# Clustered attention and a squared-ReLU feed-forward on one core: first pair on other banks and a second load queue, query-half ends given precedence, down products in another order

## The chip, the core and the metric

The kernel runs on one core of a Trainium2 chip. The metric is the device time of one execution, in microseconds (us). The core has five engines with queues of their own, which are served in order and meet only through semaphores: TensorE (PE; its weight loads are shown apart as PEld), VectorE (DVE), ScalarE (ACT), GpSimd (POOL) and SyncE (SP), which here only issues DMAs. TensorE writes its results to PSUM, a small memory of eight banks.

## The reference

Attention over 4 batches, 8 heads, 768 positions, 64 dimensions. A query sees a key only where both lie nearest to the same of 16 centroids of their head. The result, heads side by side, is the input (3072 x 512) of a feed-forward with a squared ReLU.

```python
q_assign = np.argmax(np.einsum('bhsd,hcd->bhsc', q_n, c_n), axis=-1)
k_assign = np.argmax(np.einsum('bhsd,hcd->bhsc', k_n, c_n), axis=-1)
mask = q_assign[:, :, :, None] == k_assign[:, :, None, :]
scores = scale * np.matmul(q, k.transpose(0, 1, 3, 2))
scores = np.where(mask, scores, -1000000000.0)
...
attn = np.exp(scores)
attn = attn / (np.sum(attn, axis=-1, keepdims=True) + 1e-09)
out = np.matmul(attn, v)
...
h = x @ w_in           # (3072, 512) @ (512, 2048)
r = np.maximum(h, 0.0)
g = r * r
return g @ w_out       # (3072, 2048) @ (2048, 512)
```

The inputs are float32. `_n` marks vectors divided by their length.

## The kernel before

**Pairs.** Two heads of a batch make a pair; there are 16 pairs (`NG`), four (`HP`) per batch. `load_qk` (L91) brings q and k of a pair with two DMAs each, one per head; all DMAs are issued on SP. `prep` (L324) prepares a pair in seven items: `turn` (L232) three times, which transposes four of the twelve 128x128 blocks of q and k on TensorE and has ACT copy them to `qkT`; `logits` (L250), the products with the normed centroids `cnT`; `route` (L263), which transposes the logits (`lt`) and finds each position's cluster on DVE (`mx`, `best`, `ids`); and two items that make the mask. In batch 0 (pairs 0 to 3) the mask is a one-hot matrix `oh`, transposed on TensorE by `turn_onehot` (L298) and added to the scores as a further product. In the other batches `spread` (L313) makes `qid` and the mask is a comparison on DVE after the exponential (L370).

**Units.** A pair has two query halves of 384 positions, a half three units of two key blocks. `scores` (L343) computes a unit's scores on TensorE and has ACT take the exponential (L364, tile `ex`); two units later (`LAG`) `times_v` (L386) multiplies by the values (`av`) and, in batch 0 and the first half, by ones (`sm`). Elsewhere POOL adds the exponentials up (`acc`), and `finish` (L403) makes `sm` from that with two small products. `finish` then takes the reciprocal (L420) on DVE, writes the half's part of `xT` (L421) and notes in `good` (L426) whether the sums were usable.

**PSUM.** `ps_sc` holds one tile of scores (four banks), `ps_av` two banks (tag `av`), `ps_f` two banks (tag `f`), which every transpose, logit and feed-forward product of the first stage shares.

**Feed-forward.** The weights are rounded while attention runs (`round_weights`, L131: two ACT, three DVE and one POOL operation for each of 32 pieces). For the halves in `PLAIN` (batches 0 and 1) `ffn` (L434) yields one product at a time, and the loop over units fills TensorE's queue with them. Batches 2 and 3 go through `ffn_pair` (L465) after attention, one batch at a time: seven products of quarters in place of eight, first for the up product (L519, width 384), then for the down product (L550, width 256, three tiles `i`). `combine` (L482) runs the seven in the order 1, 6, 2, 7, 5, 4, 3 and has DVE add them into the four results. For the down product, operand `g_s` of numbers 5 and 6 is made on DVE from the squared activations (L540, L473). Each tile `i` gives two blocks of the output, h=0 and h=1, each stored with one DMA of 256 KB (L561).

**Order.** The code is written for a scheduler that keeps program order except where `high_priority(offset)` moves instructions ahead, and that chooses among ready instructions of an engine by priority. So an engine's queue is not simply the program's order. `together` (L79) keeps products that can share TensorE's array side by side. The main loop (L606 on) goes over the 48 units: `scores`, `times_v` of two units before, weight rounding, fill, items of the next pair's `prep`, and `finish` where a half ends.

**End.** `check_sums` (L659) condenses `good` to one flag, after batch 2's `ffn_pair`. All engines load the flag (L698) and branch (L699) to a slow general path, which these inputs never take.

Of the kernel before, what the change touches and what calls it, by code (L numbers as in the profile page):

```python
# [8 lines left out]
F32 = mybir.dt.float32  # L9
# [15 lines left out]
def kernel(  # L25
# [50 lines left out]
    def bank(name, shape):  # L76
        return ps_f.tile(shape, F32, name=name, tag="f")

    def together(products, offset=2000):  # L79

        products = iter(products)
        nc.tensor.matmul(**next(products))  # L82
        with tc.high_priority(offset=offset):
            for product in products:
                nc.tensor.matmul(**product)  # L85
# [5 lines left out]
    def load_qk(pair):  # L91
        if pair >= NG:
            return
        b, hp = divmod(pair, HP)
        raw[pair] = []
        for name, src in (("q_raw", q), ("k_raw", k)):
            t = loads.tile([P, NCH, 2 * D], F32, name=name, tag="qk")
            for e in range(2):
                nc.sync.dma_start(
                    t[:, :, D * e : D * (e + 1)],  # L100
                    src[b, 2 * hp + e].rearrange("(p j) d -> p j d", p=P),
                )
            raw[pair].append(t)
# [53 lines left out]


    cen = once_early.tile([P, D], F32, name="cen")
    nc.sync.dma_start(cen, centroids.rearrange("h c d -> (h c) d"))  # L160
    load_qk(0)
    load_qk(1)

# [20 lines left out]
    def centroids_norm():  # L184
        sq = once_early.tile([P, D], F32, name="cen_sq")
        ss = const.tile([P, 1], F32, name="cen_ss")
        nc.vector.tensor_tensor(out=sq, in0=cen, in1=cen, op=ALU.mult)
        nc.vector.reduce_sum(out=ss, in_=sq, axis=AX.X)
        nc.vector.tensor_scalar_max(out=ss, in0=ss, scalar1=1e-30)
        nrm = const.tile([P, 1], F32, name="cen_nrm")  # L190
        nc.scalar.sqrt(nrm, ss)
        warm = once_early.tile([P, 1], F32, name="warm")
        nc.scalar.activation(out=warm, in_=nrm, func=ACT.Exp, scale=0.0)
        for _ in range(2):
            r = small.tile([P, 1], F32, name="cen_r")
            nc.vector.reciprocal(out=r, in_=nrm)
            twice = small.tile([P, 1], F32, name="cen_twice")
            nc.vector.scalar_tensor_tensor(
                out=twice, in0=ss, scalar=r, in1=nrm, op0=ALU.mult, op1=ALU.add
            )  # L200
            nc.vector.tensor_scalar_mul(out=nrm, in0=twice, scalar1=0.5)
        nc.vector.tensor_scalar_add(out=nrm, in0=nrm, scalar1=1e-6)
        rden = const.tile([P, 1], F32, name="cen_rden")
        nc.vector.reciprocal(out=rden, in_=nrm)
        row_i = const.tile([P, 1], I32, name="row_i")
        nc.gpsimd.iota(row_i, pattern=[[0, 1]], base=0, channel_multiplier=1)
        nc.vector.tensor_scalar(
            out=row_i, in0=row_i, scalar1=C, scalar2=None, op0=ALU.bitwise_and
        )
        odd = const.tile([P, 2], F32, name="odd")  # L210
        nc.vector.tensor_scalar(
            out=odd[:, 1:2], in0=row_i, scalar1=1.0 / C, scalar2=None, op0=ALU.mult
        )
        nc.vector.tensor_scalar(
            out=odd[:, 0:1], in0=odd[:, 1:2], scalar1=-1.0, scalar2=1.0, op0=ALU.mult, op1=ALU.add
        )
        for e in range(2):
            nc.vector.tensor_scalar(
                out=cn[:, e], in0=cen, scalar1=rden, scalar2=odd[:, e : e + 1],
                op0=ALU.mult, op1=ALU.mult,  # L220
            )
        pt = bank("pt", [P, P])
        nc.tensor.transpose(out=pt, in_=cn.rearrange("p e d -> p (e d)"), identity=ident)
        nc.vector.tensor_copy(out=cnT, in_=pt)

# [23 lines left out]

    def logits(pair):  # L250
        hp = pair % HP
        lg = bank("lg", [P, TB])
        together(
            dict(
                out=lg[32 * g : 32 * g + 32], lhsT=cnT[:, 2 * C * hp : 2 * C * (hp + 1)],
                rhs=qkT[pair][:, NB * g : NB * (g + 1)], start=True, stop=True,
            )
            for g in range(4)
        )
        lgs[pair] = rbp.tile([P, TB], F32, name="lgs", tag="rb")  # L260
        nc.scalar.copy(out=lgs[pair], in_=lg)
# [3 lines left out]
            number(pair)  # L265

    def number(pair):
        lt = bank("lt", [P, NB, P])
        src = lgs.pop(pair)
        for i in range(NB):  # L270
            nc.tensor.transpose(out=lt[:, i], in_=src[:, i * P : (i + 1) * P], identity=ident)
        n = NB * P // C
        lt = lt.rearrange("p i (g c) -> p (i g) c", c=C)
        mx = small.tile([P, n], F32, name="mx")
        nc.vector.reduce_max(out=mx, in_=lt, axis=AX.X)
        best = once.tile([P, n, C], BF16, name="best", tag="b")
        nc.vector.tensor_tensor(
            out=best, in0=lt, in1=mx.unsqueeze(2).to_broadcast([P, n, C]), op=ALU.is_ge
        )

        nc.vector.tensor_tensor(
            out=best, in0=best, in1=order.unsqueeze(1).to_broadcast([P, n, C]), op=ALU.mult
        )
        ids[pair] = idp.tile([P, NB, 4, 2], F32, name="ids")
        first = ids[pair].rearrange("p i g e -> p (i g e)")
        nc.vector.reduce_max(out=first, in_=best, axis=AX.X)
        if pair < HP:
            nc.vector.tensor_tensor(
                out=oh.rearrange("p i g e c -> p (i g e) c")[:, :, 0:C], in0=best,
                in1=first.unsqueeze(2).to_broadcast([P, n, C]), op=ALU.is_equal,  # L290
            )
            qid[pair] = [None, idp.tile([P, 2, S], BF16, name="ohT", tag="qid")]
        else:
            qid[pair] = [small.tile([P, NB, 2, 2], BF16, name="ids_b"),
                         idp.tile([P, 2, 2, TB], BF16, name="qid", tag="qid")]
            nc.vector.tensor_copy(out=qid[pair][0], in_=ids[pair][:, :, 0:2])

    def turn_onehot(pair, which):  # L298
        pt = ps_f.tile([P, NCH, P], BF16, name="po", tag="f")
        for c in range(NCH):  # L300
            nc.tensor.transpose(
                out=pt[:, c],
                in_=oh[:, c % NB, 2 * which + c // NB].rearrange("p e c -> p (e c)"),
                identity=ident_b,
            )
        dst = qid[pair][1][:, which]
        src = pt.rearrange("p c n -> p (c n)")
        if which == 0:
            nc.scalar.copy(out=dst, in_=src)
        else:  # L310
            nc.scalar.activation(out=dst, in_=src, func=ACT.Copy, bias=-BIG, scale=BIG)
# [153 lines left out]
    def ffn_pair(pools, b):  # L465
# [6 lines left out]
        def sub(out, a, b, eng=nc.vector):  # L472
            eng.tensor_tensor(out=out, in0=a, in1=b, op=ALU.subtract)  # L473
# [5 lines left out]
        t3 = x[0][1]  # L479
        g = gp.tile([P, FT, 2, TB], F32, name="g")  # L480

        def combine(c, product, width):  # L482

            (c11, c12), (c21, c22) = c

            def add(j, *results):
                bank = bk(width)
                product(j, bank)
                for out, to in results:
                    nc.vector.tensor_tensor(out=out, in0=bank, in1=to, op=ALU.add)  # L490

            bank = bk(width)
            product(1, bank)
            nc.scalar.copy(out=c11, in_=bank)
            add(6, (c12, c11))
            add(2, (c11, c11))
            add(7, (c21, c12))
            add(5, (c22, c21), (c12, c12))
            bank = bk(width)
            product(4, bank)  # L500
            sub(c21, c21, bank)
            add(3, (c12, c12))

        for i in range(F2):
# [31 lines left out]
        for i in range(NB):  # L536
# [19 lines left out]

            osb = [later["out"].tile([P, DM], F32, name="osb") for _ in range(2)]
            c = [[osb[h][:, M2 * m : M2 * (m + 1)] for m in range(2)] for h in range(2)]
            combine(c, product, M2)
            for h in range(2):  # L560
                nc.sync.dma_start(out_view[b, h * NB + i], osb[h])  # L561

# [31 lines left out]
    to_round = iter(range(len(weights)))  # L596
    loaded = iter(range(len(weights)))
    centroids_norm()
    for item in prep(0):
        item()  # L600
    load_v(0)
    ahead = []
# [3 lines left out]
    for u in range(len(units) + LAG):  # L606
# [35 lines left out]
        fill_steps(share - share // 2)  # L642
        if done:
            pair, h = done
            finish(pair, h)
            b, hp = divmod(pair, HP)
            if h == 1:
                for d in (qkT, ids, qid):
# [40 lines left out]
    for b in range(B):  # L689
        if (b, 0) not in PLAIN:  # L690
            ffn_pair(pools, b)
            if w_sums is not None:
                w_sums = None
                check_sums()
    fast.close()
    keep.close()

    again = nc.values_load(flag[0:1, 0:1], min_val=0, max_val=1)  # L698
    with tc.If(again != 0):  # L699
        general_path(  # L700
            tc, q, k, v, out, w_in, w_out, cn, ident, order
# [186 lines left out]
```

## Time and profile before

| | |
|---|---|
| time, median of 3 runs | 1078.52 us (1078.18 to 1081.37) |
| the profiled run | 1078.8 us, span of its records 1076.7 us |
| granted TensorE clock, mean | 0.993 |
| attention with batches 0 and 1 of the feed-forward | 7.5 to about 775 us |
| `ffn_pair` of batch 2, of batch 3 | about 775 to 925 us, 925 to 1071 us |
| DMA: read, written | 37.26 MB, 6.29 MB |

In a list in order of time, each line gives start and duration in us, engine, line of the kernel, operation, what is written <- what is read, shapes and count; in brackets the idle time of the engine before it and what ended that wait. A name with a q (SPq) is the engine's instruction queue, where DMA issues and branches are found. Ends of products on TensorE are modelled, and one float32 product leaves two records.

### The profile page before, as it was taken

The numbers are of one execution on the slowest core, as the hardware profiler recorded it, in microseconds if no ns is written. First come the engines' busy times: TensorE is split into PE (matmuls) and PEld (weight loads), VectorE is DVE, ScalarE is ACT, GpSimd is POOL, SyncE is SP. The second block draws the span as 40 slices with busy tenths as digits, with TensorE's granted clock in tenths as the row PEclk, the third lists the DMA queues.
The fourth block names the chain that finished last, engine by engine and source line by source line (L and its number), as shares of the span: only waits on it lengthen the run. The fifth ranks groups of instructions, "written<-read, shape, count | busy, mean of one in ns | idle before, by whom it ended". The sixth has DMA issues, their size and how long they took to land. (4 is left out here: it accounts for less than half of the span.)

```text
span 1076.7 us, 11238 instructions
## 1 busy us (share of the span) xinstructions
PE 1044.7 (97%) x4419; PEld 546.6 (51%) x4419; DVE 698.1 (65%) x928; ACT 296.1 (28%) x402; POOL 371.9 (35%) x245
## 2 busy tenths in 40 slices
PE   6999899999999999999999999999999899999997
PEld 3444444444444443444443344443455688655886
DVE  2666988656798865689775578976476633366521
ACT  4656454222333331333322242321011100111000
POOL 1234865333444443345344334444143200132000
PEclk9999999999999999999999999999999999999999
DMA  8654332102011020201102000000000000000000
GB/s 211 168 165 133 113 97 80 44 10 54 12 43 44 1 54 10 54 15 30 44 1 54 10 25 2 15 1 11 19 1 0 1 20 20 20 0 1 10 30 23
DMA packets 63885, 44.36 MB, mean 41 GB/s; under 512 B 51536, under 2 KB 56656, under 8 KB 63824
## 3 DMA queue, kind: packets, MB, share of 16 engines
q1 hardware_dynamic: 63824, 43.56, 14.3%
q8 instruction: 37, 0.61, 0.2%
q14 instruction: 24, 0.20, 0.1%
HBM read 37.26 MB, written 6.29 MB: 40 GB/s over the span
## 5 line engine op out<-in xcount | busy, mean ns | idle before, releaser
L370 DVE SCALAR_TENSOR_TENSOR ex<-qid,ids,ex 128x384 f32<-128x384 bf16 x288 | 248.0, 920 | 96.1 <-ACT ex L364 96.0
L382 POOL TENSOR_TENSOR acc<-acc,ex 128x768 f32<-128x768 f32 x112 | 219.0, 1955 | 244.9 <-DVE ex L370 230.3
L364 ACT ACTIVATE ex<-sc 128x1536 f32<-128x1536 f32 x96 | 139.3, 1452 | 238.1 <-PE sc L85 238.1
L439 PE MATMUL ph<-xT,w_in 128*128 128x384 f32 x512 | 187.1, 503 | 4.0 <-DVE rb L420 3.9
L452 PE MATMUL po<-w_out,gT 128*128 128x512 f32 x384 | 180.4, 605 | 0.0
L85 PE MATMUL sc<-qkT 64*128 64x384 f32 x576 | 153.0, 504 | 0.0
L85 PE MATMUL av<-ex,v_raw 128*64 128x384 f32 x576 | 144.9, 496 | 0.0
L439 PEld LDWEIGHTS ph<-xT,w_in 128*128 128x128 f32 x512 | 91.3, 190 | 89.4 <-issue 37.5
L452 PEld LDWEIGHTS po<-w_out,gT 128*128 128x128 f32 x384 | 67.8, 190 | 88.2 <-issue 87.1
L420 DVE RECIPROCAL rb<-sm 128x384 f32<-128x384 f32 x32 | 81.6, 2550 | 25.4 <-PE sm L85 25.4
L82 PE MATMUL sc<-qkT 64*128 64x384 f32 x192 | 88.0, 539 | 1.5 <-ACT ex L364 1.5
L380 POOL TENSOR_TENSOR acc<-ex 128x768 f32<-128x768 f32 x28 | 52.5, 1876 | 97.2 <-DVE ex L370 92.3
L490 DVE TENSOR_TENSOR g<-bank,g 128x384 f32<-128x384 f32 x96 | 51.8, 554 | 48.1 <-PE bank L519 48.0
L82 PE MATMUL av<-ex,v_raw 128*64 128x384 f32 x192 | 82.5, 512 | 0.0
L85 PEld LDWEIGHTS sc<-qkT 64*128 64x128 f32 x576 | 66.3, 188 | 27.9 <-issue 4.2
L473 POOL TENSOR_TENSOR w_s<-w_in 128x256 f32<-128x256 f32 x16 | 12.5, 782 | 154.7 <-PE bank L519 154.7
L447 DVE TENSOR_TENSOR gT<-gT 128x384 f32<-128x384 f32 x64 | 58.9, 931 | 10.2 <-ACT gT L446 10.0
L490 DVE TENSOR_TENSOR osb<-bank,osb 128x256 f32<-128x256 f32 x36 | 14.7, 422 | 77.2 <-PE bank L550 70.9
L550 PE MATMUL bank<-w_out,g 128*128 128x256 f32 x288 | 64.4, 379 | 0.0
L85 PEld LDWEIGHTS av<-ex,v_raw 128*64 128x64 f32 x576 | 45.9, 136 | 34.4 <-issue 33.6
L446 ACT ACTIVATE gT<-ph 128x384 f32<-128x384 f32 x64 | 31.4, 491 | 109.6 <-PE ph L439 109.5
L550 PEld LDWEIGHTS bank<-w_out,g 128*128 128x128 f32 x288 | 54.7, 190 | 7.9
(118 smaller groups left out, 1188.1 us busy)
## 6 DMA issues: line engine op xcount, KB each, us to landing
w_raw<-in_moe_w_in_dram SPq DMA_DIRECT2D x16, 512.0 KB, 4.1
w_raw<-in_moe_w_out_dram SPq DMA_DIRECT2D x16, 512.0 KB, 3.4
v_raw<-in_v_dram SPq DMA_DIRECT2D x20, 384.0 KB, 3.7
q_raw<-in_q_dram SPq DMA_DIRECT2D x32, 192.0 KB, 3.5
k_raw<-in_k_dram SPq DMA_DIRECT2D x32, 192.0 KB, 3.9
out_dram<-osb SPq DMA_DIRECT2D x24, 256.0 KB, 2.0
cen<-in_centroids_dram SPq DMA_DIRECT2D x1, 32.0 KB, 1.9
```

The costliest lines, as they stand in the source:

```text
L82: nc.tensor.matmul(**next(products))
L85: nc.tensor.matmul(**product)
L364: last_exp[0] = nc.scalar.activation(out=t, in_=sc.rearrange("p i e n -> p (i e) n")[:, :, 0:TB], func=ACT.Exp, scale=SCALE).ins
L370: nc.vector.scalar_tensor_tensor(out=to, in0=qid[pair][1][:, h, e], scalar=ids[pair][:, ch % NB, 2 + ch // NB, e : e + 1], in1=to, op0=ALU ...
L380: nc.gpsimd.tensor_tensor(out=acc[pair, h], in0=t[:, 0:2], in1=t[:, 2:4], op=ALU.add)
L382: nc.gpsimd.tensor_tensor(out=acc[pair, h], in0=acc[pair, h], in1=t[:, 2 * i : 2 * i + 2], op=ALU.add)
L420: nc.vector.reciprocal(out=rb, in_=sm)
L439: nc.tensor.matmul(ph, lhsT=w_in[:, kk, f * P : (f + 1) * P], rhs=xT[b, h][:, kk], start=(kk == 0), stop=(kk == KT - 1),)
L447: nc.vector.tensor_tensor(out=gT[f], in0=gT[f], in1=gT[f], op=ALU.mult)
L452: nc.tensor.matmul(po, lhsT=gT[f][:, i * P : (i + 1) * P], rhs=w_out[:, f], start=(f == 0), stop=(f == FT - 1),)
L490: nc.vector.tensor_tensor(out=out, in0=bank, in1=to, op=ALU.add)
L550: nc.tensor.matmul(bank, lhsT=operands[j][0][:, f], rhs=operands[j][1][:, f], start=(f == 0), stop=(f == F2 - 1),)
```

## The change

- The first pair's PSUM tiles (centroid turn, logits, `lt`, one-hot turns) come from `ps_av` (`first_bank`) instead of `ps_f`; its three `turn` items stay on `ps_f`.
- The centroid load and the first pair's two k loads are issued on ACT's queue.
- The centroid transpose leaves `centroids_norm` and runs as `centroids_turned`, between the third `turn` item and `logits` of pair 0. The warming exponential reads `ss` instead of `nrm`.
- The first one-hot copy of pair 0 goes from ACT to DVE.
- `finish` is issued under `high_priority(offset=1000)`.
- `combine` takes a list `early`: for the down products, numbers 2 and 4 are issued right after number 1, and their results wait in their banks. The order is 1, 2, 4, 6, 7, 5, 3.
- The store of h=1 stands ahead of h=0's in the program, and the very last tile of h=0 is stored in two column halves.
- `values_load` of the flag moves to directly after `check_sums`.

```diff
@@ -76,6 +76,10 @@
     def bank(name, shape):
         return ps_f.tile(shape, F32, name=name, tag="f")

+    def first_bank(name, shape, dtype=F32):
+
+        return ps_av.tile(shape, dtype, name=name, tag="av")
+
     def together(products, offset=2000):

         products = iter(products)
@@ -96,7 +100,7 @@
         for name, src in (("q_raw", q), ("k_raw", k)):
             t = loads.tile([P, NCH, 2 * D], F32, name=name, tag="qk")
             for e in range(2):
-                nc.sync.dma_start(
+                (nc.scalar if pair == 0 and src is k else nc.sync).dma_start(
                     t[:, :, D * e : D * (e + 1)],
                     src[b, 2 * hp + e].rearrange("(p j) d -> p j d", p=P),
                 )
@@ -157,7 +161,7 @@


     cen = once_early.tile([P, D], F32, name="cen")
-    nc.sync.dma_start(cen, centroids.rearrange("h c d -> (h c) d"))
+    nc.scalar.dma_start(cen, centroids.rearrange("h c d -> (h c) d"))
     load_qk(0)
     load_qk(1)

@@ -189,8 +193,9 @@
         nc.vector.tensor_scalar_max(out=ss, in0=ss, scalar1=1e-30)
         nrm = const.tile([P, 1], F32, name="cen_nrm")
         nc.scalar.sqrt(nrm, ss)
+
         warm = once_early.tile([P, 1], F32, name="warm")
-        nc.scalar.activation(out=warm, in_=nrm, func=ACT.Exp, scale=0.0)
+        nc.scalar.activation(out=warm, in_=ss, func=ACT.Exp, scale=0.0)
         for _ in range(2):
             r = small.tile([P, 1], F32, name="cen_r")
             nc.vector.reciprocal(out=r, in_=nrm)
@@ -219,7 +224,9 @@
                 out=cn[:, e], in0=cen, scalar1=rden, scalar2=odd[:, e : e + 1],
                 op0=ALU.mult, op1=ALU.mult,
             )
-        pt = bank("pt", [P, P])
+
+    def centroids_turned():
+        pt = first_bank("pt", [P, P])
         nc.tensor.transpose(out=pt, in_=cn.rearrange("p e d -> p (e d)"), identity=ident)
         nc.vector.tensor_copy(out=cnT, in_=pt)

@@ -249,7 +256,7 @@

     def logits(pair):
         hp = pair % HP
-        lg = bank("lg", [P, TB])
+        lg = (bank if pair else first_bank)("lg", [P, TB])
         together(
             dict(
                 out=lg[32 * g : 32 * g + 32], lhsT=cnT[:, 2 * C * hp : 2 * C * (hp + 1)],
@@ -265,7 +272,7 @@
             number(pair)

     def number(pair):
-        lt = bank("lt", [P, NB, P])
+        lt = (bank if pair else first_bank)("lt", [P, NB, P])
         src = lgs.pop(pair)
         for i in range(NB):
             nc.tensor.transpose(out=lt[:, i], in_=src[:, i * P : (i + 1) * P], identity=ident)
@@ -296,7 +303,10 @@
             nc.vector.tensor_copy(out=qid[pair][0], in_=ids[pair][:, :, 0:2])

     def turn_onehot(pair, which):
-        pt = ps_f.tile([P, NCH, P], BF16, name="po", tag="f")
+        if pair == 0:
+            pt = first_bank("po", [P, NCH, P], BF16)
+        else:
+            pt = ps_f.tile([P, NCH, P], BF16, name="po", tag="f")
         for c in range(NCH):
             nc.tensor.transpose(
                 out=pt[:, c],
@@ -305,7 +315,9 @@
             )
         dst = qid[pair][1][:, which]
         src = pt.rearrange("p c n -> p (c n)")
-        if which == 0:
+        if which == 0 and pair == 0:
+            nc.vector.tensor_copy(out=dst, in_=src)
+        elif which == 0:
             nc.scalar.copy(out=dst, in_=src)
         else:
             nc.scalar.activation(out=dst, in_=src, func=ACT.Copy, bias=-BIG, scale=BIG)
@@ -479,26 +491,36 @@
         t3 = x[0][1]
         g = gp.tile([P, FT, 2, TB], F32, name="g")

-        def combine(c, product, width):
+        def combine(c, product, width, early=()):
+
+

             (c11, c12), (c21, c22) = c

-            def add(j, *results):
+            waiting = {}
+
+            def bank_of(j):
+                if j in waiting:
+                    return waiting[j]
                 bank = bk(width)
                 product(j, bank)
+                return bank
+
+            def add(j, *results):
+                bank = bank_of(j)
                 for out, to in results:
                     nc.vector.tensor_tensor(out=out, in0=bank, in1=to, op=ALU.add)

             bank = bk(width)
             product(1, bank)
             nc.scalar.copy(out=c11, in_=bank)
+            for j in early:
+                waiting[j] = bank_of(j)
             add(6, (c12, c11))
             add(2, (c11, c11))
             add(7, (c21, c12))
             add(5, (c22, c21), (c12, c12))
-            bank = bk(width)
-            product(4, bank)
-            sub(c21, c21, bank)
+            sub(c21, c21, bank_of(4))
             add(3, (c12, c12))

         for i in range(F2):
@@ -556,9 +578,12 @@

             osb = [later["out"].tile([P, DM], F32, name="osb") for _ in range(2)]
             c = [[osb[h][:, M2 * m : M2 * (m + 1)] for m in range(2)] for h in range(2)]
-            combine(c, product, M2)
-            for h in range(2):
-                nc.sync.dma_start(out_view[b, h * NB + i], osb[h])
+            last = b == B - 1 and i == NB - 1
+            combine(c, product, M2, early=(2, 4))
+
+            for h in (1, 0):
+                for cols in (slice(0, M2), slice(M2, DM)) if last and h == 0 else (slice(0, DM),):
+                    nc.sync.dma_start(out_view[b, h * NB + i][:, cols], osb[h][:, cols])

@@ -596,7 +621,9 @@
     to_round = iter(range(len(weights)))
     loaded = iter(range(len(weights)))
     centroids_norm()
-    for item in prep(0):
+    for i, item in enumerate(prep(0)):
+        if i == 3:
+            centroids_turned()
         item()
     load_v(0)
     ahead = []
@@ -642,7 +669,8 @@
         fill_steps(share - share // 2)
         if done:
             pair, h = done
-            finish(pair, h)
+            with tc.high_priority(offset=1000):
+                finish(pair, h)
             b, hp = divmod(pair, HP)
             if h == 1:
                 for d in (qkT, ids, qid):
@@ -692,10 +720,10 @@
             if w_sums is not None:
                 w_sums = None
                 check_sums()
+                again = nc.values_load(flag[0:1, 0:1], min_val=0, max_val=1)
     fast.close()
     keep.close()

-    again = nc.values_load(flag[0:1, 0:1], min_val=0, max_val=1)
     with tc.If(again != 0):
         general_path(
             tc, q, k, v, out, w_in, w_out, cn, ident, order
```

## Prediction

> **What bounds the kernel now.** I read the engine totals first, then the waits of TensorE, then the order of time around each long wait, and last the end of the run.
>
> ```profile
> span 1076.7 us, 11238 instructions
> PE 1044.7 (97%) x4419; PEld 546.6 (51%) x4419; DVE 698.1 (65%) x928; ACT 296.1 (28%) x402; POOL 371.9 (35%) x245
> ...
> PE pt L223 <- DVE cen_n L218: 7.5, 1, 7.5
> PE pb L318 <- DVE ids_b L296: 4.1, 7, 2.1
> PE ph L439 <- DVE rb L420: 3.9, 1, 3.9
> PE po L301 <- DVE oh L288: 3.5, 2, 2.3
> PE bank L550 <- DVE g_s L473: 3.2, 2, 2.9
> ...
> PE pb L318 <- DVE rb L420: 1.1, 2, 0.6
> ```
>
> TensorE is busy for 97% of the span, so the number and form of its products set the time; no edit changes those. The waits (engine, line, waited for: total us, times, longest) are what a reordering can win: all of TensorE's idle time is some 32 us, 7.5 of it at the start and 5.8 after its last product. The next lines, in order of time, place them.
>
> ```profile
> 2.57 1.34 SPq L99 DMA_DIRECT2D k_raw<-in_k_dram  x2
> 7.53 0.45 PE L223 MATMUL pt<-ident,cen_n 128*128 128x128 f32 x1 [7.53 <-DVE cen_n L218]
> 17.63 1.28 PE L301 MATMUL po<-ident_b,oh 128*128 128x128 bf16 x12 [2.26 <-DVE oh L288]
> 21.07 1.45 ACT L364 ACTIVATE ex<-sc 128x1536 f32<-128x1536 f32 x1 [0.17 <-PE sc L85]
> 32.99 0.84 PE L301 MATMUL po<-ident_b,oh 128*128 128x128 bf16 x12 [1.20 <-DVE oh L288]
> ...
> 126.80 2.54 DVE L420 RECIPROCAL rb<-sm 128x384 f32<-128x384 f32 x1
> 129.39 4.45 PE L439 MATMUL ph<-xT,w_in 128*128 128x384 f32 x8 [3.92 <-DVE rb L420]
> ...
> 854.18 5.35 PE L550 MATMUL bank<-w_t,g_s 128*128 128x256 f32 x16 [2.86 <-DVE g_s L473]
> 1001.54 3.72 PE L550 MATMUL bank<-w_t,g_s 128*128 128x256 f32 x16 [0.38 <-DVE g_s L473]
> 1070.91 0.42 DVE L490 TENSOR_TENSOR osb<-bank,osb 128x256 f32<-128x256 f32 x1 [3.03 <-PE bank L550]
> ...
> 854.00:856.00 2.00, 1.82 (x4) 1.51 (x5) 2.00 (x3) 0.00 (x0) 0.00 (x0) 0.53 0.00 0
> ```
>
> The first product runs at 7.53 because the centroid turn is at the head of TensorE's queue. At 854.18 the second product of the first down block waits 2.86 us for `g_s`, and sixteen records then take 5.35 us where the same sixteen take 3.62 elsewhere: the last line (columns: busy time of PE, weight load, DVE, ACT, POOL, then granted clock, DMA share, GB/s) shows a clock of 0.53 behind that wait.
>
> **What the Trainium skill says.** "TensorE: Matmul & The Clock Gate", Part 1, says that the clock halves after an idle window of some 3.4 us and comes back after a busy one, the windows running freely. The trace agrees: 0.5 from 854.1 to 857.5, so an idle of 2.86 us costs a further 5.35 - 3.62 = 1.73 us. "DMA: Bandwidth & Descriptors", Issuing engines are not separate DMA queues, says that issuing from several engines saves only issue time, as the same 16 DMA engines move all. The trace agrees in so far as these are full (mean busy share about 1.0 to 1.3 per us from 3 to 9 us, at 197 to 249 GB/s). The same page, Latency and other measured facts, puts a register load from memory at about 600 ns; the trace has 0.54 us for DVE's load of the flag at 1070.9.
>
> **The change, part by part.** I compared the queue of every engine in both kernels; durations are of the profiled execution, whose span is 1076.7 us. It was timed at 1078.8 us, and the three timed runs have 1078.18, 1078.52 and 1081.37. I work out savings on the span and take them off 1078.5.
>
> *Down products.* The queue becomes 1, 2, 4, 6, 7, 5, 3. Products 2 and 4 read raw quarters, so after product 1 there are two more blocks of 3.45 us (starts at 859.37 and 862.82) before product 6 needs `g_s`. Product 1 starts at 847.70, so product 6 comes at about 847.70 + 3 x 3.45 = 858.1; `g_s` ends at 852.92 + 1.21 = 854.1. The wait goes, and so does the cold clock. The in-place subtraction into the quarter that product 2 reads must follow that product (done about 854.6) and precede product 3, two blocks and more later. Saved: 2.86 + 1.73 at 854, and 0.38 + (3.72 - 3.62) at 1001, together 5.1 us. The additions are the same in number. Two banks are held longer, hidden by there being eight. Bounds 4 to 5.3.
>
> *First pair.* Removed ahead of the first transposes: the wait for `cen_n` (7.53) and one issue on SP (0.39 us for the centroids). Moved to ACT's queue: the centroid load and both k loads, 0.39 + 1.34 = 1.7 us of issue ahead of its table load, which was idle until 3.37; `cen_nrm` comes some 0.4 us later, but DVE's L201 no longer waits 1.10 us for `warm`, so `cen_n` is about 0.6 us earlier, and now nothing waits for it. On SP, the loads of pair 1 and v come forward 1.7 us, and with the DMA engines full they share with k. So I do not credit k with arriving earlier: it lands at 3.25 + 4.1 = 7.35 before (issue plus landing time) and I put it at 7.3, bounds 6.6 to 7.8. The six q transposes (1.3 us cold) now run in front of that, so k's are done at about 8.9 instead of 10.6. The centroid turn, four score products and the logits follow; the logits are copied at about 12.0 to 12.8 (13.25 before), and the first exponential, 21.07 before, comes at about 19.3: 1.8 saved. Two further gains: in the wait for `oh` TensorE now does pair 1's transposes, logits (1.0 us at 24.39) and `lt` (0.5), and nine of the twelve turns of pair 1's one-hot (0.6) come before the third scores, without the idle 1.20 at 32.99. Against this: those turns stand ahead of the second scores in TensorE's in-order queue and wait for a DVE chain with one more copy in it (`ohT`, about 0.8 us as on ACT), some 0.7 us. Sum: 1.8 + 1.0 + 0.5 + 0.6 + 1.2 - 0.7 = 4.4, rounded to 4.3; bounds 0 (k late, clock cold again) and 6. TensorE has no long wait between 33 and 125 us, so this reaches the end.
>
> *Ends of query halves.* `finish` is a reciprocal (2.54) and two products (0.55 each), 3.64 us of DVE, now ahead of masks in 24 or so halves. I looked for what it unblocks. The reciprocal at 126.80 sits behind the same four DVE instructions as before (three roundings, one `gT`): the boost does not pass it forward there, so I keep the 3.92 wait. In the later pairs it passes two masks, which should remove the two `pb` waits for `rb` (0.48 at 188.50, 0.59 at 405.80): 1.0 us. The sum products move up to five `po` products earlier (5 x 0.43 = 2.2 us), against 6.95 us between the last `acc` and its sum product in the tightest half (119.86), so they should not stall TensorE. The masks that wait for it have some 8 us in hand (one unit's end at 319.5, its values at 327.4). Bounds: -1 to 5.5.
>
> *Ends.* `values_load` keeps its place: on PE, DVE, ACT and POOL it is still directly before the last branch, on SP still before the last six tiles' stores. Of the stores, h=1 already went first; new is the last tile in halves. The final store is issued at 1071.36 and takes about 2.0 us to land, so 1073.4; SP's branch at 1071.7 is followed by its semaphores only at 1074.7. A store half the size is hidden by that: 0, bounds -0.5 to +0.3.
>
> Sum: 5.1 + 4.3 + 1.0 = 10.4; 1078.5 - 10.4 = 1068.1 us.
>
> **The rivals.**
>
> *The boost bites at 125 us too.* If DVE is ahead of its backlog there (it is busy for 5.30 of 5.30 us from 124.0), the wait of 3.92 and its cold clock (4.45 for eight records, against 8 x 0.345 + 0.15 = 2.9, so 1.6) go: 1068.1 - 5.5 = 1062.6. Against it: DVE's unchanged queue order. Chance 0.17.
>
> *The start gives nothing.* k lands late behind pair 1's q, or pair 1's turns hold the second scores: DMA engines that were already full speak for it. Then 1078.5 - 5.1 - 1.0 = 1072.4. Chance 0.17.
>
> *Slower: the masks come too late.* DVE is in order; 3.64 us of `finish` stand ahead of up to four masks, and the values products and POOL's `acc` wait for masks. It decides once the 8 us in hand of a half fall below 3.64; if half of 24 halves then lose 1.5 us each, 18 us are lost: 1068.1 + 18 = 1086. Against it: TensorE waits for masks only 0.8 us in all before (the weight load of `av`). Chance 0.05.
>
> *It does not do what it says,* in part: the early flag and the half store are worth nothing by the queues, and that is in my forecast. All of it void, 1078: chance 0.06.
>
> **How the numbers follow.** Forecast 1068.1, chance 0.55; its own range, from the bounds above, is 1064.5 to 1071.5. The range for 8 in 10 takes in the first rival and most of the second: 1061 to 1074. A measurement of this kernel can tell about 0.3%, 3.2 us, from no change. Faster by more: 0.55 + 0.17 + 0.17, less a little of the second rival's tail, 0.88; within: 0.07; slower: 0.05.
>
> **What would show it.** In the profile after: sixteen records of product 6 at 3.6 us with no wait for `g_s` and clock 1.00 near 850; first transposes before 7 us, first exponential near 19.3, no `oh` wait near 30; a `ph` wait for `rb` near 121 to 125 still about 3.9; the same 5.8 us from the last product to the end. I am wrong if TensorE waits for `ex` or for POOL's `acc`, or if the first exponential is not earlier than 20.5.

## The result and the profile after

The kernel after takes 1066.49 us (median of four runs, 1063.85 to 1067.89), the kernel before 1079.94 in the same series. The ratio is 0.9873, 95% interval [0.9842, 0.9904]: 13.7 us off 1080, where 10.4 was forecast; the time of 1066.49 is inside the range and 1.6 us from the 1068.1 forecast. Part by part the forecast was less good than its sum: one term was three to four times too small.

The page of after, and its waits of TensorE (engine, line, waited for: total us, times, longest):

```profile
span 1065.7 us, 11238 instructions
PE 1041.3 (98%) x4419; PEld 544.5 (51%) x4419; DVE 693.7 (65%) x929; ACT 295.9 (28%) x401; POOL 370.7 (35%) x245
...
PE pt L245 <- DMA q_raw<-in_q_dram: 6.2, 1, 6.2
PE pb L330 <- DVE ids_b L303: 4.9, 7, 2.1
PE ph L451 <- DVE rb L432: 3.3, 1, 3.3
PE po L311 <- DVE oh L295: 1.4, 1, 1.4
```

The waits for `cen_n`, for `g_s` and of `pb` for `rb` are gone, that for `oh` is down from 3.5 to 1.4 us, that of `ph` for `rb` from 3.9 to 3.3. All waits in that view fell from 25.7 to 18.4 us, the span by 11.0: the rest must lie in TensorE's busy time, which fell by 3.4 although its products are the same.

After in order of time, at the places shown of before:

```profile
6.18 1.51 PE L245 MATMUL pt<-ident,q_raw 128*128 128x128 f32 x6 [6.18 <-DMA q_raw<-in_q_dram]
...
19.52 1.45 ACT L376 ACTIVATE ex<-sc 128x1536 f32<-128x1536 f32 x1 [0.59 <-PE sc L89]
20.83 0.68 PE L311 MATMUL po<-ident_b,oh 128*128 128x128 bf16 x9 [1.36 <-DVE oh L295]
...
119.22 2.54 DVE L432 RECIPROCAL rb<-sm 128x384 f32<-128x384 f32 x1
121.82 5.49 PE L451 MATMUL ph<-xT,w_in 128*128 128x384 f32 x8 [3.27 <-DVE rb L432]
...
852.78 3.62 PE L572 MATMUL bank<-w_t,g_s 128*128 128x256 f32 x16
...
1060.21 0.42 DVE L512 TENSOR_TENSOR osb<-bank,osb 128x256 f32<-128x256 f32 x1 [2.37 <-PE bank L572]
```

The first exponential comes at 19.52 (forecast 19.3), the down block runs through at 3.62 us per sixteen records, and from the last add to the end it is 5.5 us (5.8 before). The long wait at 121.82 has stayed.

The view by windows of after (busy PE, PEld, DVE, ACT, POOL, then granted clock, DMA share, GB/s) adds what that wait does to the clock here, and that the clock is full at the down block:

```profile
121.00:123.00 2.00, 1.18 (x2) 0.84 (x3) 1.97 (x5) 0.00 (x0) 1.92 (x2) 0.50 0.61 231
123.00:125.00 2.00, 2.00 (x4) 1.01 (x3) 1.97 (x2) 0.00 (x0) 1.48 (x1) 0.50 0.08 31
125.00:127.00 2.00, 2.00 (x4) 0.67 (x2) 2.00 (x4) 0.00 (x0) 1.09 (x1) 0.50 0.00 0
...
854.00:856.00 2.00, 2.00 (x11) 1.76 (x10) 0.00 (x0) 0.00 (x0) 0.00 (x0) 1.00 0.00 0
```

To see where the time went, I matched the 96 exponentials of each kernel one by one. The table gives how far each traced run is ahead of before (us) at four of them, named by their start in before, and at the last add, which before reaches at 1070.91. The rows from e1 on are the runs of the next sections. A lead is that of one traced execution, which can lie off the median of its kernel's runs: 1.4 us above it for after, 3.3 for e7, 2.9 for e11, 1.7 below it for e3.

| kernel | 42.8 | 84.3 | 135.8 | 743.7 | last add |
|---|---|---|---|---|---|
| after | 2.6 | 8.0 | 6.3 | 5.3 | 10.7 |
| e1 finish alone | -0.4 | 5.0 | 4.6 | 3.6 | 5.2 |
| e2 start alone | 3.0 | 3.1 | 3.1 | 3.2 | 3.4 |
| e3 down alone | 0.2 | 0.2 | 0.2 | 0.2 | 5.6 |
| e4 after without finish | 2.4 | 2.5 | 2.5 | 2.6 | 8.0 |
| e5 higher precedence in before | -2.3 | -1.2 | -2.0 | -2.0 | -1.8 |
| e6 eight groups split | 4.0 | 9.4 | 9.0 | -6.3 | -0.9 |
| e7 finish higher still | 2.7 | 8.1 | 6.5 | -3.1 | 2.3 |
| e8 rounding put off | 2.8 | 8.3 | 12.0 | 13.2 | 18.6 |
| e9 one queue | 3.2 | 8.6 | 9.9 | 8.9 | 14.3 |
| e10 old ends | 3.3 | 8.8 | 10.0 | 9.0 | 14.4 |
| e11 whole groups in before | -2.0 | -0.8 | -2.0 | -2.3 | -2.3 |
| e12 put off and whole groups | 2.1 | 7.8 | 11.4 | 11.5 | 16.9 |

After gains 2.6 us at the start, then 5.4 between 43 and 84 us, where the prediction had nothing, loses 1.7 around the wait at 121.82 and 1.0 more by 743.7, where the prediction had its 1.0 for `finish`, and gains 5.4 in the down products.

### The profile page after: what moved, and what is told of

It is laid out like the page before. It is cut to its first block, busy times and chain, and to the rows that moved or that the text cites. A ratio compares the mean times of both kernels' runs of the same rounds, so it can differ in the third digit from the quotient of the medians.

```text
span 1065.7 us, 11238 instructions
## 1 busy us (share of the span) xinstructions
PE 1041.3 (98%) x4419; PEld 544.5 (51%) x4419; DVE 693.7 (65%) x929; ACT 295.9 (28%) x401; POOL 370.7 (35%) x245
## 4 chain that ended last, share of the span: by engine, by line
PE 92%; DVE 5%; ACT 1%; issue 1%; DMA 0%; SPq 0%; ACTq 0%; DVEq 0%
PE po L464 16%; PE ph L451 15%; PE bank L541 14%; PE bank L572 14%; PE sc L86 7%; PE av L86 6%; PE sc L89 6%; PE av L89 5%; PE pt L245 2%; PE sm L86 2%; PE sm L89 1%; PE pb L330 1%; DVE w_raw L156 1%; DVE w_out L149 1%; PE lg L86 1%
## 5 line engine op out<-in xcount | busy, mean ns | idle before, releaser
L382 DVE SCALAR_TENSOR_TENSOR ex<-qid,ids,ex 128x384 f32<-128x384 bf16 x288 | 239.4, 889 | 115.2 <-ACT ex L376 115.1
```

Of the source, the lines that this page charges most:

```text
L382: nc.vector.scalar_tensor_tensor(out=to, in0=qid[pair][1][:, h, e], scalar=ids[pair][:, ch % NB, 2 + ch // NB, e : e + 1], in1=to, op0=ALU ...
```

## The parts one by one (e1 to e4)

The suspect for 43 to 84 us was `finish`. The reading at this point: TensorE's queue of before breaks up products that could stand side by side, after's does so less.

**e1.** Before, with

```diff
-            finish(pair, h)
+            with tc.high_priority(offset=1000):
+                finish(pair, h)
```

> The kernel before with one edit of the change: the ends of query halves (the call of finish) take precedence in the order. Nothing of the computation is left out. Theory (products kept together): before, score products and logits that could stand side by side on the array are split by work that is slipped between them; with this edit the kept-together groups of the pairs after the first come back, and the time is 4 to 5 us below before, with a lead of about 5 us over before that arises between 42 and 82 us and with fewer lone score products of 0.84 us in that stretch. Rival (the prediction's own sizing): only the two waits for rb at 188 and 406 us go, 1.0 us below before, and nothing between 42 and 82 us.

Measured: ratio 0.9961 [0.9949, 0.9974], 4.2 us below before (2.8 to 5.5). The lead of 5.4 us arises between 43 and 84 us, as in after; at 743.7 it has come down to 3.6. The 1.6 that the table has on top of that at the last add is not `finish`'s. The wait for `g_s` is there as in before, but the sixteen records behind it take 3.72 us and not 5.35, and the clock is full there:

```profile
850.58 3.72 PE L550 MATMUL bank<-w_t,g_s 128*128 128x256 f32 x16 [2.87 <-DVE g_s L473]
```

**e2.** Before, with the first pair's part of the diff alone (`first_bank`, the second queue, `centroids_turned`, `warm` from `ss`, the first one-hot copy on VectorE).

> The kernel before with the first pair's other banks, its second load queue, the centroids turned later and the first one-hot copy on VectorE; finish, down products and stores as before. Nothing is left out. Theory (read from the trace after): the lead of the start is 2.3 to 2.7 us by 42 us and stays there, 2 to 3 us below before. Rival (the prediction): 4.3 us below before. A second rival: the start is also what brings the lead between 42 and 82 us, then 7 to 8 us below before.

Measured: 0.9962 [0.9949, 0.9975], 4.1 us. The traced lead is 3.0 us by 43 us and stays. In the other kernels that have the new start it is 2.1 to 4.0 by then. Both sizes are inside the interval; the second rival is out.

**e3.** Before, with `combine(c, product, M2, early=(2, 4))` and the diff's `combine`.

> The kernel before with the down products' order alone changed (products 2 and 4 issued ahead of 6). Nothing is left out. Theory: the wait of 2.86 us for g_s at the start of the first down block and the stretch at half clock behind it go, with the smaller pair at 1001 us: 5.1 to 5.4 us below before. Rival: the wait moves to another product of the block, or the clock dips there anyway: 2 us or less.

Measured: 0.9965 [0.9952, 0.9978], 3.8 us; in the trace 5.4 us, all of it after the 743.7 mark. The trace of before has the slow stretch behind the wait for `g_s`, that of e1 does not; where it is absent, some 5.4 - 1.6 = 3.8 us are to be won (an estimate from these two traces). How many executions of before have it is not known.

**e4.** After, with the edit of e1 taken back.

> The kernel after with finish at its old precedence, all else of the change kept. Nothing is left out. Theory (products kept together by the precedence of finish): 4 to 6 us above the kernel after, so 7 to 9 us below before, with a lead over before of about 3 us at 82 us in place of 8. Rival (the prediction's sizing): 1.0 us above the kernel after, so about 12 us below before.

Measured: 0.9911 [0.9896, 0.9925], 4.1 us more than after by the ratios, and the lead at 84 us is 2.5 in place of 8.0. After's own interval is 3.3 us to each side, so this difference alone says little; against e9 and e10 below, which have after's `finish`, e4 is 4.5 and 5.4 above. By 743.7 the traces give less: 3.6 in e1, 2.7 between after and e4. So `finish` is worth some 3 to 4 us, and the rival's 1.0 is too small: e1's interval shuts it out. The three parts sum to 12.1 us of the 13.7; the intervals hold the difference.

**What `finish` gives back.** Between 136 and 744 us the two `pb` waits for `rb` are gone, and e1's lead rises by 0.6 and 0.7 there. It falls all the same, by 1.0, as after's does, and e4's does not fall. A place where it falls, in before and in e1:

```profile
714.67 3.60 PE L452 MATMUL po<-w_out,gT 128*128 128x512 f32 x8
...
710.68 1.02 PE L452 MATMUL po<-w_out,gT 128*128 128x512 f32 x2
711.63 0.54 PE L82 MATMUL sm<-acc,ups 128*64 128x384 f32 x1
...
712.42 2.84 PE L452 MATMUL po<-w_out,gT 128*128 128x512 f32 x6
```

In before the sum products `sm` follow the eight `po` records at 718.20; in e1 they come earlier and stand among them, and by starts the eight take 0.95 + 2.78 = 3.73 us in place of 3.53. After 133 us before has `sm` right ahead of the next scores in 14 halves, e1 in 4. Ten such places would make some 2.0 us (an estimate from this one), against the 1.3 that the two waits give. No run tests this.

## What finish moves (e5, e11, e7, e6)

The order of time of before, second pair of the stretch. A float32 product leaves two records in these rows, so x2 is one product and x4 are two:

```profile
64.98 0.91 PE L82 MATMUL sc<-qkT 64*128 64x384 f32 x2 [0.25 <-ACT ex L364]
65.82 0.84 PE L85 MATMUL lg<-qkT,cnT 128*32 128x384 f32 x4
...
66.34 2.55 DVE L420 RECIPROCAL rb<-sm 128x384 f32<-128x384 f32 x1
66.59 0.92 PE L85 MATMUL sc<-qkT 64*128 64x384 f32 x4
...
71.08 0.55 DVE L421 SCALAR_TENSOR_TENSOR xT<-av,rb 128x384 f32<-128x384 f32 x1
...
72.54 4.09 PE L85 MATMUL sm<-ex,ups 128*64 128x384 f32 x24
76.56 0.91 PE L85 MATMUL sc<-qkT 64*128 64x384 f32 x2
```

One score product alone takes 0.91 us, two side by side 0.92. "TensorEngine Tiling (Array Packing)", Key Properties, in the Trainium skill says that different tiles of the array work in parallel; these two rows agree. In before a pair's logits stand as 2 and 2, one unit's scores as 1, 2, 1, the next unit's as 3 and 1 around the twelve products of `sm`.

The same stretch of e1:

```profile
64.06 2.55 DVE L420 RECIPROCAL rb<-sm 128x384 f32<-128x384 f32 x1
...
66.66 0.54 PE L82 MATMUL av<-ex,v_raw 128*64 128x384 f32 x1 [0.19 <-DVE rb L420]
...
66.93 0.54 DVE L421 SCALAR_TENSOR_TENSOR xT<-av,rb 128x384 f32<-128x384 f32 x1
...
68.00 4.04 PE L85 MATMUL sm<-ex,ups 128*64 128x384 f32 x24
```

Two things differ. From one pair's `av` to the next takes 17.85 us (48.81 to 66.66) in place of 20.71 (48.37 to 69.08). By start times, of these 2.86 us the scores as 3 and 1 make 0.92 (1.48 + 0.84 against 1.40), the logits 0.71 (0.83 + 0.77 against 0.89), the 1, 2, 1 about 0.8, the waits 0.2. And on VectorE `xT` follows the reciprocal's start after 2.87 us, not 4.74: it has passed four instructions, two that make `best` and two of the rounding. The reciprocal and `xT` are the last readers of the two banks of tag `av`; the next pair's `av` and `sm` need them. In before `sm` starts at 72.54, behind `xT`'s end at 71.63; in e1 at 68.00, behind 67.47. So either could be the cause: broken groups, or the bank.

**e5.** Before, with groups held together more strongly:

```diff
-    def together(products, offset=2000):
+    def together(products, offset=6000):
```

> The kernel before with finish untouched; only the precedence of the products that are to stand together is raised (offset 6000 in place of 2000). In TensorE's queue this keeps the four score products ahead of the 12 products of sums together in the second and third pair (3 and 1 in before), leaves the first group of those pairs at 1 and 3, and splits one group of av products per pair into 3 and 1. Nothing is left out. Theory (a split group is what costs): 2 times 0.92 us less for the score products, some tenths back for av, so a lead of 1.3 to 3 us over before that arises between 42 and 82 us, with no edit of finish. Rival (it is the earlier reciprocal on VectorE that pays): no lead there, time as before.

Measured: 0.9996 [0.9987, 1.0005], no change. Between 43 and 84 us it gains 1.2 us, just short of what was expected. Of this the groups make 0.2: twice 0.92 for whole score groups, less twice 0.8 for an `av` group that now stands as 3 and 1 (1.44 + 0.79 us against 1.42). Waits for the exponential are 0.6 less. At the start it loses 2.3, as scores stand ahead of `lt` there. Too mixed to decide.

**e11.** Before, with whole groups and nothing newly broken:

```diff
-        together(products)
+        together(products[:4], 20000)
+        if products[4:]:
+            together(products[4:])
```

> The kernel before with finish untouched and its reciprocals at the same places in VectorE's queue; only the four score products of a unit are a group of their own (offset 20000), apart from the four one-hot ones. In TensorE's queue no score group of the first four pairs is broken up any more, and no av group either, unlike in the run with offset 6000. Nothing is left out. Theory (broken-up groups cost, finish only happened to close them up): a lead over before of 4 to 6 us that arises by 82 us, as with the finish edit. Rival (the earlier place of finish itself pays): less than 1.5 us.

Measured: 0.9989 [0.9979, 0.9998], 1.2 us. In the trace the lead grows by 1.2 us between 43 and 84 us, from -2.0 to -0.8: the rival's number, though not by its reasons alone. The order of time of e11:

```profile
62.29 0.59 PE L82 MATMUL sc<-qkT 64*128 64x384 f32 x1 [0.58 <-ACT ex L366]
...
66.58 0.59 PE L82 MATMUL sc<-qkT 64*128 64x384 f32 x1 [0.52 <-ACT ex L366]
...
67.46 2.55 DVE L422 RECIPROCAL rb<-sm 128x384 f32<-128x384 f32 x1
...
70.06 0.54 PE L82 MATMUL av<-ex,v_raw 128*64 128x384 f32 x1 [1.01 <-DVE rb L422]
...
72.20 0.55 DVE L423 SCALAR_TENSOR_TENSOR xT<-av,rb 128x384 f32<-128x384 f32 x1
...
74.28 4.09 PE L85 MATMUL sm<-ex,ups 128*64 128x384 f32 x24
```

No group is broken, yet the pair takes 20.34 us (49.72 to 70.06). The time that was lost in lone products is now lost in waits: 0.58 and 0.52 for the exponential, as there is one tile of scores only, and 1.01 for `rb`. `xT` still comes 4.74 us after the reciprocal's start, and `sm`, the long filler, behind it. So my theory of broken groups falls as a full account. What fits all three kernels is that in before the queue has to fill the time until the bank is free, with lone products or with waits, and that the `finish` edit frees the bank 1.87 us earlier, so that the twelve `sm` products can stand where they fill a gap. That is argued from these rows; a kernel that moves `xT` alone was not run.

**e7.** After, with `high_priority(offset=2500)` around `finish`.

> The kernel after with the precedence of finish raised further (offset 2500 in place of 1000). TensorE's queue is the same up to 330 us; in four later places a group of four score products then stands as 1 and 3, and the ffn products around it in other pieces. Nothing is left out. Theory (what pays is groups kept whole, not the precedence): 4 times 0.92, so 3 to 4.5 us above the kernel after, lost step by step at those four places. Rival (an earlier finish pays in itself): as the kernel after or up to 1 us below it.

Measured: 0.9925 [0.9912, 0.9938], 5.6 us above after; in the trace the loss is 8.4 us at the last add and comes in four steps of about 2.2. Each has a group as 1 and 3 (0.92) and, not expected, a wait of about 1.1:

```profile
345.23 0.91 PE L86 MATMUL sc<-qkT 64*128 64x384 f32 x2
...
350.89 0.33 PE L330 MATMUL pb<-ident_b,ids_b 128*128 128x128 bf16 x3 [0.98 <-DVE rb L432]
```

An earlier `finish` is no gain in itself here. The `pb` waits for `rb` that the change removed come back when its precedence goes further.

**e6.** After, with one group of four scores broken in each of eight halves:

```diff
+        apart = pair in (5, 8, 11, 14) and c == 2
-        together(products)
+        together(products[:3] if apart else products)
+        if apart:
+            return lambda: exps(pair, h, c, sc, products[3:])
+        exps(pair, h, c, sc, [])
...
+        if u < len(units) and rest:
+            rest()
```

Here `exps` is the rest of `scores`, with the product it is given ahead of the exponential; the loop calls `rest()`, what `scores` returned, behind `times_v`.

> The kernel after with eight groups of four score products split on purpose, in the third pair of heads' later pairs (5, 8, 11, 14, both halves): three products in their place, the fourth behind the av products that follow. Nothing is left out or added. Theory: three products 1.48 us and a lone one 0.84 in place of four in 1.40, 0.92 us for each group, 7.4 us above the kernel after. Rival (a split costs only what a product takes, and the array catches up): within 1 us of the kernel after.

Measured: 0.9998 [0.9989, 1.0007], 13.5 us above after. Between the marks of 135.8 and 743.7 us its lead falls by 15.3 us, after's by 1.0. The lone product:

```profile
236.64 0.59 PE L86 MATMUL sc<-qkT 64*128 64x384 f32 x1
...
240.59 2.84 PE L472 MATMUL po<-w_out,gT 128*128 128x512 f32 x6
243.36 0.91 PE L382 MATMUL sc<-qkT 64*128 64x384 f32 x2
244.20 1.98 PE L472 MATMUL po<-w_out,gT 128*128 128x512 f32 x4
```

From 243.36 to 244.20 it keeps the array for 0.84 us, as expected. The other half of the loss is a wait that had not been expected: `pb` for `ids_b` goes from 4.9 us to 11.1, 6.2 more. 7.4 and 6.2 make 13.6, where the runs have 13.5 and the trace, by 743.7, 14.2. So breaking a group costs its 0.92 and, in the places chosen here, nearly as much again in waits for VectorE.

## The wait at 121.82 (e8, e12)

The prediction kept this wait. What it is worth was its first rival's price, 5.5 us.

**e8.** After, with one unit's rounding put off:

```diff
-        rounding += 4
+        rounding += 0 if u in (15,) else 4
```

> The kernel after with one unit's share of weight rounding put off by a unit (unit 15 rounds nothing), so that one w_out chunk stands behind the reciprocal of 119 us in VectorE's queue and not ahead of it. Nothing is left out. If the wait of 3.27 us for rb at 121.8 us and the stretch at half clock behind it reach the end: the reciprocal starts some 5 us earlier, the wait goes, the eight ffn products take 3.1 us and not 5.5, and the time is 4 to 6 us below the kernel after. Rival: the wait only moves (to the next ffn bank, to pb at 171 us, or to w_out at 191 us), and less than 2 us is left.

Measured: 1059.86 us, 0.9809 [0.9796, 0.9822], 6.9 us below after and 20.6 below before.

```profile
111.53 2.03 DVE L149 TENSOR_SCALAR w_out<-w_out 128x512 f32<-128x512 f32 x1
113.59 1.91 DVE L153 TENSOR_SCALAR w_out<-w_out 128x512 uint32<-128x512 uint32 x1
115.42 0.70 DVE L156 SCALAR_TENSOR_TENSOR w_raw<-w_raw 128x512 uint32<-128x512 uint32 x1
116.02 0.54 DVE L459 TENSOR_TENSOR gT<-gT 128x384 f32<-128x384 f32 x1
116.49 2.54 DVE L432 RECIPROCAL rb<-sm 128x384 f32<-128x384 f32 x1
...
119.09 2.85 PE L451 MATMUL ph<-xT,w_in 128*128 128x384 f32 x8 [0.82 <-DVE rb L432]
```

The reciprocal starts 2.7 us earlier (expected 5; one piece of rounding still stands right ahead of it), the wait is 0.82 in place of 3.27, and the eight records take 2.85 in place of 5.49. The rounding's two simple steps take 2.03 and 1.91 us here. In after the same kind of step takes 0.42 at another time:

```profile
113.85 4.08 POOL L394 TENSOR_TENSOR acc<-acc,ex 128x768 f32<-128x768 f32 x2
114.23 2.03 DVE L149 TENSOR_SCALAR w_out<-w_out 128x512 f32<-128x512 f32 x1
...
125.74 0.42 DVE L149 TENSOR_SCALAR w_out<-w_out 128x512 f32<-128x512 f32 x1
```

After's trace has 64 such steps (`TENSOR_SCALAR` on 128x512). The 38 that started while GpSimd was idle took 0.43 us at most; the 26 that started while one of its instructions ran took 0.43 to 2.05, 1.7 in the median. The Trainium skill's "SBUF — State Buffer", SBUF: two separate sides, says that GpSimd and VectorE steps of certain kinds lock each other out of a shared pair of ports for whole instructions. The durations agree; no run here shows that these steps are of such a kind. So a queue of cheap steps ahead of the reciprocal is dear where POOL is busy.

Part of the 6.9 us is the clock, at two places. The view by windows of e10 (a kernel with after's order at this place) has the same wait, 3.25 us at 121.04, and no slow stretch behind it:

```profile
121.00:123.00 2.00, 1.96 (x6) 1.25 (x7) 1.98 (x4) 0.00 (x0) 1.92 (x2) 1.00 0.62 238
123.00:125.00 2.00, 2.00 (x11) 0.98 (x11) 1.97 (x4) 0.49 (x1) 0.71 (x1) 1.00 0.00 0
125.00:127.00 2.00, 2.00 (x16) 0.58 (x10) 2.00 (x3) 1.19 (x1) 1.41 (x1) 1.00 0.00 0
```

After's profile has clock 0.50 from 121.0 to 127.8 instead and falls 2.9 us further behind e10 there (0.8 us behind at the exponential ahead of it, 3.7 at the one after). The Trainium skill's "TensorE: Matmul & The Clock Gate", Part 1, says that the clock's windows of some 3.4 us run freely. That a wait of about that length then may or may not fill one is a reading that the two profiles fit; no run tests it.

The second place is behind the wait of `pb` for `ids_b`, which is 0.4 us shorter in e8. In order, after and e8:

```profile
170.89 0.51 PE L330 MATMUL pb<-ident_b,ids_b 128*128 128x128 bf16 x6 [2.14 <-DVE ids_b L303]
...
164.65 0.51 PE L330 MATMUL pb<-ident_b,ids_b 128*128 128x128 bf16 x6 [1.71 <-DVE ids_b L303]
```

After's clock is 0.50 from 172.2 to 175.6, e8's is full, and e8's lead over after grows by 2.2 us between the exponentials of 158.6 and 182.1. The wait's length alone does not decide it: in eleven traces a wait of 2.13 to 2.15 us there is followed by 3.4 us at half clock, e12's of 2.72 is not. The page has the clock halve after an idle window of some 3.4 us; these waits are shorter, and the traces decide. Against after's trace e8 gains 7.9 us at the last add: 0.3 at the start, 5.4 at the first place, 2.2 at the second. Against e10's, which has no slow stretch at the first place, it gains 4.1.

**e12.** e8, with the edit of e11.

> The kernel after with unit 15's weight rounding put off by a unit and the score products as a group of their own. Against the run with the put-off alone only the last broken groups of the third pair (logits 2 and 2, score products 1, 2, 1, near 42 us) are closed up. Nothing is left out. Theory: 1.0 to 1.8 us below the run with the put-off alone, so 7.5 to 8.5 us below the kernel after. Rival: 0, the place is bound by the exponential before it.

Measured: 1062.14 us, 0.9836 [0.9822, 0.9849]: 2.3 us above e8, where 1.0 to 1.8 below was expected. TensorE's wait of `av` for `rb` is now 1.5 us in all, that for `ids_b` 5.5 in place of 4.5. Closing the broken group at 42 us takes e12 from 0.8 us behind e8 to 0.9 ahead by the exponential of 48.5 us, but by that of 84.3 it is 0.5 behind again: the group had been filling a wait. e8 is the best of these kernels.

## The parts forecast at nothing (e9, e10)

**e9.** After, with

```diff
-                (nc.scalar if pair == 0 and src is k else nc.sync).dma_start(
+                nc.sync.dma_start(
...
-    nc.scalar.dma_start(cen, centroids.rearrange("h c d -> (h c) d"))
+    nc.sync.dma_start(cen, centroids.rearrange("h c d -> (h c) d"))
```

> The kernel after with the first pair's k and the centroids loaded from SyncE's queue again; the other banks, the order of the start, finish, down products and stores as after. Nothing is left out. The prediction credited the second queue with 0.05 us (k's last block 7.35 to 7.3 us): within 1 us of the kernel after, the first transposes of q not later than 6.7 us. Rival (the second queue is what carries the start): 2 us or more above the kernel after, and the lead over before at 42 us under 1 us.

Measured: 0.9869 [0.9852, 0.9887], as after. The first transposes start at 5.84 (6.18 in after) and wait 0.31 us for k at 7.66. The second queue is worth nothing that can be seen; the start's gain is that of the banks, of the order and of the copy on VectorE, which were not run apart.

**e10.** After, with `for h in range(2)`, whole stores, and `values_load` behind the two `close` calls.

> The kernel after with the ends put back: stores of a block in the old order and whole, the flag's values_load at its old place. Nothing is left out. The prediction put these at 0 (bounds -0.5 to +0.3): within 0.5 us of the kernel after, and 5.5 to 5.8 us from the last add to the end. Rival (the half store or the early flag read takes something off the end): 0.3 us or more above the kernel after in the stretch behind the last add.

Measured: 0.9861 [0.9844, 0.9877], as after; 5.7 us from the last add to the end, 5.5 in after. Over all traces it is 5.7 to 5.8 in the seven kernels with the old ends and 5.3 to 5.8, 5.4 in the mean, in the seven with the new ones: 0.2 to 0.3 us, if anything.

## Why the prediction was right and wrong

- *Down products, 5.1.* Right: 5.4 us in the traces of after and e3, 3.8 in e3's runs with 5.1 inside the interval. The wait and the slow clock behind it are both gone. But "an idle of 2.86 us costs a further" 1.73 holds for some executions only: in e1's trace the same wait costs its 2.87 and no more.
- *First pair, 4.3.* Right in kind, somewhat large: 3.0 us in e2's trace, 2.6 in after's, 4.1 in e2's runs. The first exponential came at 19.52 (19.3), 1.6 us earlier where 1.8 was said. What fell short is "two further gains" and the turns set against them, together 1.0 in after's trace where the sum has 2.6: the turns wait for DVE 1.36 us in place of 0.7, and behind that after's clock is 0.5 from about 22 to 25.4 us. Nothing credited to the second queue: right (e9).
- *Ends of query halves, 1.0.* Mis-sized, and this is the term that failed: some 3 to 4 us (4.2 in e1's runs, 3.6 in its trace by 743.7). Both `pb` waits went as said (0.6 and 0.7 in the lead), but the stretch that holds them gives nothing in all, as the lead falls by 1.0 there. The gain is elsewhere: "I looked for what it unblocks" looked at TensorE's waits and at the place of one reciprocal. Most of the loss was in no row of waits: TensorE was busy there, with products at half the array. The prediction had "the sum products move up to five `po` products earlier" and gave it no price but a stall. What the edit moved in the first pairs was `xT`, from 4.74 to 2.87 us behind the reciprocal, and with it the bank that the next pair's sums need; that this is the cause is argued, not shown. "TensorE has no long wait between 33 and 125 us" was true and did not mean that nothing could be won there. The bound of 5.5 did reach that far.
- *The wait at 125.* Right: "the boost does not pass it forward there". The first rival had the price about right (5.5; e8 found 4.1 to 6.9) and the mechanism wrong. Its time, 1062.6, is not what came.
- *Ends, 0.* Right within 0.3 (e10).
- *The start gives nothing* is out by e2. *Masks too late* is out: behind the first pair no product of TensorE waits for a mask or for POOL's `acc`, and one waits 0.2 us for the exponential; only the waits of `pb` for `ids_b`, from which masks are made, rose, by 0.8 us.

That the time came within 1.6 us is in part luck. The saving is off by about 3: the oversized start and the undersized `finish` partly offset each other, and `finish` gives some of its gain back. The rest is that the forecast starts from 1078.5, while before took 1079.94 in the series of the result.

## What to carry to other kernels

A busy engine can hide a loss that no view of waits shows: where small products share an array, compare the duration of a row of two with that of a row of one, and count the groups in the queue. But closing a group is a gain only if the work behind it is ready (e11, e12); look for the bank or tile that the filler needs and for the instruction that frees it, on whichever engine that is. When work with slack stands ahead of an instruction that TensorE waits for, putting it off by one step of the loop can be worth more than a reordering by precedence.

## What the runs showed of the hardware that was not expected

- A score product of 64 rows alone takes as long (0.91 us) as two side by side (0.92).
- A wait of 3.27 us was followed by 6.8 us at half clock in one profile, one of 3.25 us at the same place by none in another; one of 2.86 us by 3.4 us at half clock in before, one of 2.87 us at the same product by none in e1.
- The same VectorE step on 128x512 took 0.42 us and, beside POOL's additions, 2.03.
- Eight records of 128x512 took 3.53 us in a row and 3.73 with two small `sm` products among them.
